# Two VectorE passes over neighbouring PSUM banks joined into one two-bank pass, with new planner seeds, in a scheduled attention and MLP kernel

## Chip, cores, metric

One core of a Trainium2 chip. The time is the device time of one execution in microseconds (us); medians of several executions are quoted. All executions here are fast (granted TensorE clock 0.997 to 1.0).

## The reference, cut

```python
def reference(A_x, A_wq, A_wk, A_wv, A_wo, B_x, B_w1, B_w2):     # x: 1 x 2048 x 512
    xn = _layernorm(A_x)
    q = (xn @ wq) as 32 heads of 16;  k = xn @ wk;  v = xn @ wv   # one k and v for all heads
    p = softmax(q k^T / 4);  s = (p v) @ wo
    g = silu(silu(xn @ w1) @ w2)                                 # F = 1792
    return x + s * g
```

## The kernel before

The kernel writes no instruction order by hand. A planner in Python places tasks on five engines one after another with assumed durations, and the instructions are emitted in the order found. What matters here:

- A **score phase** is up to four row-tiled score matmuls side by side, each filling one PSUM bank with a slot of 128 keys x 512 (head, query) columns. Seven banks rotate.
- A slot goes one of two ways. ScalarE takes the exp of one to three neighbouring banks in one call, and TensorE then needs one probability-times-V matmul. Or VectorE makes 16-bit exponents from one bank (the "pass"), GpSimd makes three shifted copies of them, and TensorE needs four such matmuls. So VectorE relieves ScalarE and loads TensorE.
- Between score phases TensorE does column-tiled work in rounds of four matmuls: P times V, the MLP, projections.
- Random numbers from ten seeds vary some limits of the planner. The seeds decide the order, and are picked for a good result.

```python
SEEDS, STRETCH, SPREAD = (2502, 4652, 1398, ...), 64, 0.3
...
        def pass_d(b, bt, g, i, kt):                 # one slot on VectorE
            tot[g, i] += K
            def placed(pop):
                pool_free.append(b)                  # the bank may be planned again
                pvq[g][i].append(...)                # and the slot's P times V
            bt.P[i] = pl.add(Task(DV, T_P, lambda v: v.tensor_scalar(
                db_sb[:, bt.b, i * NQ:(i + 1) * NQ], bank(b), 128.0 * LOG2E, 128.0 * (SHIFT_BETA + 127.0),
                op0=ALU.mult, op1=ALU.add), [("ps", b)], [("Db", bt.b, i)], 0, on_place=placed))
...
        def do_S(t):                                 # one score phase
            banks = [b for r, b in bank_times() if r <= t + 30][:4]
            ...                                      # dslots for VectorE, sl for ScalarE
            for b, d in zip(dbanks, dslots):
                pass_d(b, *d)
```

The softmax here doesn't subtract the row's maximum and nothing guards it: scores larger than these inputs give would overflow.

## Time and profile before

| | before |
|---|---|
| time, median of 2 | 669.83 us |
| span of the profiled run | 668.0 us |
| busy TensorE, ScalarE, VectorE, GpSimd | 99%, 98%, 92%, 84% |
| score phases / passes on VectorE | 640 / 736 |

Two lines besides those that the prediction shows. The group of score matmuls (columns: line, engine, operation, count; busy us and mean ns; idle time before them and who ended it):

```profile
L866 PE MATMUL ps<-qt_sb,kt_sb 32*128 32x512 bf16 x2048 | 250.7, 384 | 3.7 <-ACT pa_sb L1717 1.1 <-DVE db_sb L1002 0.5 <-DVE kt_sb L567 0.4
```

And the last score phase in the timeline (start us, length us):

```profile
657.37 0.10 PEld L866 LDWEIGHTS ps<-qt_sb,kt_sb 32*128 32x128 bf16 x3 [0.42 <-issue]
```

The steady stretch thus ends at 657.4 us, and 10.6 us of tail follow.

### The profile page before, as it was taken

What the parts mean: (1) busy time and instruction counts of PE and PEld (TensorE: products, weight loads), DVE (VectorE), ACT (ScalarE), POOL (GpSimd) and SP (SyncE); (2) the same over time, 40 slices, a digit from 0 to 9 for tenths busy, and PEclk for the clock granted to TensorE, in tenths of its full rate; (3) what the DMA queues carried; (4) which work ended last, traced back from release to release, by engine and by line L of the source; (5) the groups of instructions that cost most, each with busy time, mean ns of one, the idle gap of its engine ahead of it and who ended that gap; (6) DMA issues with size and microseconds to landing.
All of it is one profiled execution on the core that took longest, in us unless ns stands there. A gap on an engine that the chain in (4) does not pass through costs nothing.

```text
span 668.0 us, 21223 instructions
## 1 busy us (share of the span) xinstructions
PE 658.0 (99%) x8962; PEld 191.2 (29%) x8963; DVE 615.0 (92%) x1093; ACT 652.1 (98%) x768; POOL 558.7 (84%) x556
## 2 busy tenths in 40 slices
PE   8999999999999999999999999999999999999997
PEld 4422222222222222222222222222222222222223
DVE  8989999899999998999998999999899999998995
ACT  6999999999999999999999999999999999999996
POOL 3059889989898899898899887999899989998972
PEclk9999999999999999999999999999999999999999
DMA  8500000000000000000000000000000000000000
GB/s 299 166 9 2 2 2 2 2 3 2 1 2 18 19 18 18 1 2 2 2 2 2 17 18 18 18 2 1 3 2 2 2 18 17 18 18 2 2 2 33
DMA packets 11821, 12.86 MB, mean 19 GB/s; under 512 B 1808, under 2 KB 11216, under 8 KB 11728
## 3 DMA queue, kind: packets, MB, share of 16 engines
q1 hardware_dynamic: 10928, 10.78, 5.0%
q8 instruction: 72, 1.18, 0.7%
q10 hardware_dynamic: 800, 0.72, 0.3%
q14 instruction: 21, 0.17, 0.1%
HBM read 8.95 MB, written 2.10 MB: 17 GB/s over the span
## 4 chain that ended last, share of the span: by engine, by line
PE 74%; ACT 17%; DVE 7%; issue 1%; DMA 0%; POOL 0%; ACTq 0%; DVEq 0%
PE ps L1282 32%; PE ps L866 25%; PE ps L511 16%; ACT pa_sb L1717 16%; DVE db_sb L1002 2%; ACT t_sb L669 1%; DVE stats_sb L458 1%; DVE u_sb L671 1%; DVE xnT_sb L538 0%; DMA ds_sb<-in_A_x_dram 0%; DVE xn_sb L487 0%; POOL ds_sb L1202 0%; DVE fin_sb L719 0%; DVE f_sb L1338 0%; DVE mv_sb L462 0%
## 5 line engine op out<-in xcount | busy, mean ns | idle before, releaser
L1202 POOL INT64_ADD ds_sb<-db_sb x544 | 553.1, 1038 | 91.6 <-DVE db_sb L1002 34.9
L1717 ACT ACTIVATE pa_sb<-ps 128x1024 bf16<-128x1024 f32 (+2 forms) x671 | 616.3, 1029 | 5.5 <-PE ps L866 3.1
L1002 DVE TENSOR_SCALAR db_sb<-ps 128x512 uint16<-128x512 f32 x736 | 475.5, 683 | 39.6 <-PE ps L866 28.6
L1282 PE MATMUL ps<-ds_sb,v_sb 128*32 128x512 bf16 x2208 | 274.4, 383 | 0.0
L866 PE MATMUL ps<-qt_sb,kt_sb 32*128 32x512 bf16 x2048 | 250.7, 384 | 3.7 <-ACT pa_sb L1717 1.1
L1282 PE MATMUL ps<-pa_sb,v_sb 128*32 128x512 bf16 x1317 | 245.8, 382 | 0.0
L1282 PE MATMUL ps<-db_sb,v_sb 128*32 128x512 bf16 x736 | 176.2, 383 | 0.0
L866 PEld LDWEIGHTS ps<-qt_sb,kt_sb 32*128 32x128 bf16 x2048 | 62.6, 90 | 275.6 <-ACT pa_sb L1717 154.5
L1282 PEld LDWEIGHTS ps<-ds_sb,v_sb 128*32 128x32 bf16 x2208 | 68.4, 95 | 60.4 <-issue 41.9
L511 PE MATMUL ps<-xnT_sb,w_sb 128*32 128x512 bf16 x896 | 71.9, 384 | 0.0
L1282 PEld LDWEIGHTS ps<-pa_sb,v_sb 128*32 128x32 bf16 x1317 | 60.7, 95 | 39.3 <-issue 26.7
L511 PE MATMUL ps<-w_sb,u_sb 128*32 128x512 bf16 x820 | 64.2, 384 | 0.0
L1282 PEld LDWEIGHTS ps<-db_sb,v_sb 128*32 128x32 bf16 x736 | 43.7, 95 | 20.3 <-issue 15.6
L669 ACT ACTIVATE t_sb<-ps 128x512 bf16<-128x512 f32 x72 | 45.2, 628 | 0.0
L671 DVE SCALAR_TENSOR_TENSOR u_sb<-t_sb,ps 128x512 bf16<-128x512 bf16 x56 | 38.3, 684 | 1.4
L618 PE MATMUL ps<-w_sb,u_sb 32*128 32x512 bf16 x76 | 29.2, 384 | 0.0
L511 PEld LDWEIGHTS ps<-xnT_sb,w_sb 128*32 128x32 bf16 x896 | 17.2, 94 | 27.3 <-issue 21.5
L511 PEld LDWEIGHTS ps<-w_sb,u_sb 128*32 128x32 bf16 x820 | 15.4, 95 | 23.0 <-issue 19.7
L1338 DVE STREAM_TRANSPOSE f_sb<-ps 128x512 f32<-128x512 f32 x31 | 21.9, 706 | 0.1
L511 PE MATMUL ps<-wo_sb,on_sb 128*32 128x512 bf16 x256 | 19.8, 383 | 0.3 <-DVE on_sb L1316 0.3
L511 PE MATMUL ps<-xnT_sb,wq_sb 128*32 128x512 bf16 x240 | 18.8, 384 | 0.0
L1342 DVE TENSOR_TENSOR otr_sb<-f_sb,rcp_sb 128x256 bf16<-128x256 f32 x31 | 12.9, 417 | 1.4 <-POOL ds_sb L1202 1.1
(75 smaller groups left out, 169.0 us busy)
## 6 DMA issues: line engine op xcount, KB each, us to landing
w_sb<-in_B_w_dram SPq DMA_DIRECT2D x2, 1792.0 KB, 14.3
xr_sb<-in_A_x_dram SPq DMA_DIRECT2D x16, 128.0 KB, 2.5
out_dram<-ob_sb SPq DMA_DIRECT2D x16, 128.0 KB, 1.7
ds_sb<-in_A_x_dram SPq DMA_DIRECT2D x3, 512.0 KB, 6.7
wq_sb<-in_A_wq_dram SPq DMA_DIRECT2D x1, 512.0 KB, 4.9
wo_sb<-in_A_wo_dram SPq DMA_DIRECT2D x1, 512.0 KB, 16.7
kt_sb<-kt_sb ACTq DMA_DIRECT2D x4, 112.0 KB, 4.2
ds_sb<-in_A_x_dram ACTq DMA_DIRECT2D x2, 128.0 KB, 2.9
```

What stands on the lines that cost most here:

```text
L458: ts_ = pl.add(Task(DV, 593.0, lambda v, t=t: v.bn_stats(stats_sb[:, t, :], x_tile(t)), [xkey(t)], [("st", t)], 1 + j, gate=(lambda j=j: S ...
L511: last = h.matmul(bank(b)[32 * j:32 * (j + 1), 0:n], lhsT=lhs(j), rhs=rhs, start=start, stop=stop, tile_position=(0, 32 * j), skip_group_c ...
L618: return (lambda pe: pe.matmul(bank(b), lhsT=lhs(k, rows, 0, P), rhs=rhs(k, rows), start=False, stop=last, tile_position=(32 * i, 0), skip ...
L669: t1 = Task(AC, 490.0, lambda a: a.activation(t_sb[:, k, :], src, ACT.Tanh, scale=scale), [held], [("t", k)], 0, [t0])
L671: t2 = Task(DV, T_P, lambda v: v.scalar_tensor_tensor(out=dst, in0=t_sb[:, k, :], scalar=1.0, in1=src, op0=ALU.add, op1=ALU.mult), [held, ...
L866: return pe.matmul(bank(b), lhsT=kt_sb[32 * i:32 * i + 32, g % 2, kt * P:(kt + 1) * P], rhs=qt_sb[32 * i:32 * i + 32, (g // 2) % NQR, :], ...
L1002: bt.P[i] = pl.add(Task(DV, T_P, lambda v: v.tensor_scalar(db_sb[:, bt.b, i * NQ:(i + 1) * NQ], bank(b), 128.0 * LOG2E, 128.0 * (SHIFT_BET ...
L1202: whole["po"].append(pl.add(Task(PO, T_P64, lambda g, cols=cols: g.int64_add(ds_sb[:, s, cols].bitcast(U64), db_sb[:, bt.b, cols].bitcast( ...
L1282: h = pe.matmul(bank(OB)[32 * i:32 * (i + 1), cols], lhsT=lhs, rhs=rhs, start=s0, stop=s1, tile_position=(0, 32 * i), skip_group_check=True)
L1338: t1 = pl.add(Task(DV, T_TR, lambda v: v.transpose(f_sb[:, k, :], bank(OB)), [("ps", OB)], [("F", k)], 1, [norm.get(("m", g - 2))]))
L1342: t3 = pl.add(Task(DV, 332.0, lambda v: v.tensor_tensor(o3[:, :, val:val + DH], f3[:, :, val:val + DH], rcp_sb[:, k, :].unsqueeze(2).to_br ...
L1717: op = pl.place(AC, 0.8333 * NQ * n + T_AF, lambda a: a.activation(pa_sb[:, s * NQ:(s + n) * NQ].rearrange("p (b n) -> p b n", n=NQ), ps3[ ...
```

## The change

The intent: VectorE pays a fixed amount per instruction. When a phase gives it two slots in neighbouring banks, one instruction reads both banks, and that amount is paid once. The seeds were changed in the same step, and the condition that starts the tail was made stricter. With joining off and the old seeds, the changed source builds into the same instructions, orders and waits as the kernel before, so the stricter condition does nothing there.

```diff
-SEEDS, STRETCH, SPREAD = (2502, 4652, 1398, 4134, 3319, 6151, 8548, 1413, 942, 5642), 64, 0.3
+SEEDS, STRETCH, SPREAD = (6371, 4628, 3818, 3584, 5044, 3525, 4965, 8747, 3685, 2283), 64, 0.3
+PAIR = 1
+        def pass_pair(b, ds):
+            bt, g = ds[0][0], ds[0][1]
+            ii = [d[2] for d in ds]
...
+            def placed(pop):
+                for k, (_, _, i, kt) in enumerate(ds):
+                    pool_free.append(b + k)
+                    pvq[g][i].append((pop, ...))
+            t = pl.add(Task(DV, 2 * T_P - 66.0, lambda v: v.tensor_scalar(
+                db_sb[:, bt.b, :].rearrange("p (i n) -> p i n", n=NQ)[:, ii[0]:ii[1] + 1:ii[1] - ii[0], :], ps3[:, b:b + 2, :],
+                128.0 * LOG2E, 128.0 * (SHIFT_BETA + 127.0), op0=ALU.mult, op1=ALU.add),
+                [("ps", b), ("ps", b + 1)], [("Db", bt.b, i) for i in ii], 0, on_place=placed))
...
-            for b, d in zip(dbanks, dslots):
-                pass_d(b, *d)
+            if PAIR and nd == 2 and dslots[0][0] is dslots[1][0] and dbanks[1] - dbanks[0] == 1:
+                pass_pair(dbanks[0], dslots)
+            else:
+                for b, d in zip(dbanks, dslots):
+                    pass_d(b, *d)
...                                        # and a stricter condition for make_tail()
```

More of the change, by code (lines that the diff above doesn't have):

```diff
@@ L1004, in pass_d @@
                 op0=ALU.mult, op1=ALU.add), [("ps", b)], [("Db", bt.b, i)], 0, on_place=placed))
+        def pass_pair(b, ds):
+            bt, g = ds[0][0], ds[0][1]
+            ii = [d[2] for d in ds]
+            for i in ii:
+                tot[g, i] += K
+            def placed(pop):
+                for k, (_, _, i, kt) in enumerate(ds):
+                    pool_free.append(b + k)
+                    pvq[g][i].append((pop, v_lhs(1, g, kt), db_sb[:, bt.b, i * NQ:(i + 1) * NQ].bitcast(BF16),
+                                      [("Db", bt.b, i)] + v_reads(1, kt), ("d", bt), None))
+            t = pl.add(Task(DV, 2 * T_P - 66.0, lambda v: v.tensor_scalar(
+                db_sb[:, bt.b, :].rearrange("p (i n) -> p i n", n=NQ)[:, ii[0]:ii[1] + 1:ii[1] - ii[0], :], ps3[:, b:b + 2, :],
+                128.0 * LOG2E, 128.0 * (SHIFT_BETA + 127.0), op0=ALU.mult, op1=ALU.add),
+                [("ps", b), ("ps", b + 1)], [("Db", bt.b, i) for i in ii], 0, on_place=placed))
+            for i in ii:
+                bt.P[i] = t
         def do_S(t):
@@ L1045, in do_S @@
             nd = len(dslots)
+            if PAIR and nd == 2 and dslots[0][0] is dslots[1][0]:
+                dslots.sort(key=lambda d: d[2])
             st["la"] = n - nd
@@ L1563, in pe_step @@
             start_jobs(t)
-            if st["assigned"] == NG * SLOTS and (MT_EARLY and not active and st["job"] == len(jobs) or st["expn"] == len(units)) and not tail["made"] and all(
+            if st["assigned"] == NG * SLOTS and (MT_EARLY and not active and st["job"] == len(jobs) and len(pool_free) + len(units) - st["expn"] == len(BANKS) or st["expn"] == len(units) and len(pool_free) == len(BANKS)) and not tail["made"] and all(
                     tt in tmp_task for tt in range(NT - 4, NT)):
```

## The prediction

> **What bounds the kernel now.** I read the engine totals first, then the busy time by stretches, then the groups kept apart by shape, then the waits, then the timeline of a steady piece.
>
> ```profile
> PE 658.0 (99%) x8962; PEld 191.2 (29%) x8963; DVE 615.0 (92%) x1093; ACT 652.1 (98%) x768; POOL 558.7 (84%) x556
> ```
>
> Three engines are nearly full, so the totals cannot say which one sets the time. From 38 to 657 us the split by stretches gives:
>
> ```profile
> 38.00:657.00 619.00, 617.39 (x8361) 172.19 (x8362) 576.51 (x960) 615.58 (x710) 553.06 (x544) 1.00 0.03 7
> ```
>
> The columns are length, then busy time of TensorE, weight loads, VectorE, ScalarE, GpSimd. TensorE and ScalarE both lack less than 4 us of 619; VectorE lacks 42 us, GpSimd 66 us. The head (38 us) and the tail (11 us) are short. TensorE's busy time is modelled, so I check it against the waits:
>
> ```profile
> PEld ps L866 <- ACT pa_sb L1717: 154.5, 364, 0.7
> PEld ps L866 <- DVE db_sb L1002: 102.4, 231, 0.8
> ```
>
> Line 866 is the score matmuls (row-tiled, one "phase" at a time), 1717 is ScalarE's exp, 1002 is VectorE's pass (scores in PSUM to 16-bit exponents), the line that the change touches. It looks as if TensorE lost 102 us to that pass. The timeline shows that it did not:
>
> ```profile
> 302.26 0.10 PEld L866 LDWEIGHTS ps<-qt_sb,kt_sb 32*128 32x128 bf16 x3 [0.42 <-ACT pa_sb L1717]
> 302.58 0.12 PEld L511 LDWEIGHTS ps<-xnT_sb,wq_sb 128*32 128x32 bf16 x8 [0.23 <-issue]
> 303.13 0.10 PEld L866 LDWEIGHTS ps<-qt_sb,kt_sb 32*128 32x128 bf16 x3 [0.42 <-ACT pa_sb L1717]
> ```
>
> The cycle is 303.13 - 302.26 = 0.87 us for one score phase and two rounds of column-tiled work. Three 512-column steps of 0.216 us are 0.65; the other 0.22 is two changes of tiling, about 0.11 each. A gap of 0.42 on the weight-load row is the last matmul streaming plus that change, not a wait. Going through the whole timeline in stretches of 4 us, 539 of 641 gaps before a score phase are exactly 0.42. Eighty exceed 0.44, by 6.5 us in all, and 5.0 of those 6.5 us stand behind the VectorE pass. **TensorE is the bound, and all its waiting before score phases is about 6.5 us, 1% of the span.**
>
> ScalarE is a close second:
>
> ```profile
> L1717 ACT ACTIVATE pa_sb<-ps 128x1024 bf16<-128x1024 f32 x624 | 591.0, 1051 | 4.4 <-PE ps L866 2.0 <-DVE rstd_sb L478 0.4 <-issue 0.3
> L1002 DVE TENSOR_SCALAR db_sb<-ps 128x512 uint16<-128x512 f32 x736 | 475.5, 683 | 39.6 <-PE ps L866 28.6 <-PE ps L618 5.4 <-POOL ds_sb L1202 1.2
> L1717 ACT ACTIVATE pa_sb<-ps 128x512 bf16<-128x512 f32 x41 | 24.7, 630 | 1.1 <-PE ps L866 1.0
> L1717 ACT ACTIVATE pa_sb<-ps 128x1536 bf16<-128x1536 f32 x6 | 8.7, 1485 | 0.0
> ```
>
> It idles 4.4 us before its 624 main calls. VectorE idles 39.6 us before its passes, mostly because the scores were not there yet.
>
> **What the Trainium skill says.** "VectorE: DVE Perf Modes", section "The TRN2 errata", puts an fp32 PSUM source at one element per cycle of 0.96 GHz and the measured fixed term of one operation at about 150 cycles: 533 + 156 = 689 ns for 512 elements. The trace's 683 agrees. But a duration is not a pitch. "Perfetto Trace Analysis", section "Optimizing Scalar/DVE Operations", says a PSUM operation's overhead as engine time is about 125 ns, the profiled latency being about twice that because the write acknowledgement overlaps the next instruction. Here the overlap is larger:
>
> ```profile
> 38.44 2.48 DVE L1002 TENSOR_SCALAR db_sb<-ps 128x512 uint16<-128x512 f32 x4
> ```
>
> Four passes in 2.48 us with the last 0.69 long: pitch (2.48 - 0.69) / 3 = 0.60 us, so the overhead per instruction is 600 - 533 = 67 ns. The measurement decides: joining two passes saves about 67 ns, not 125 or 150. "TensorEngine Tiling (Array Packing)", "Key Properties", says that changing the tiling mode drains the engine; the 0.11 us per change above agrees.
>
> **The change, part by part.** The order of both programs' instructions gives the counts; no time is in it.
>
> VectorE: 736 single passes become 616 single and 64 joined (40 with adjacent outputs, 24 with outputs strided by whole slots), so slots on VectorE go from 736 to 616 + 128 = 744. Joining saves 64 x 67 = 4.3 us. Eight more slots cost 8 x 0.60 = 4.8 us. Whole-batch shifts on VectorE fall from 8 to 4: 4 x 0.6 = 2.4 us less. Sum: about -1.9 us of 615, on an engine with some 40 us idle.
>
> GpSimd: shifts 544 to 554, 10 x 1.04 = +10.4 us, into 91.6 us of idle before them. Free.
>
> ScalarE: exp slots fall from 2048 - 736 = 1312 to 1304. From the rows (1485 - 630) / 1024 = 0.835 ns per element, so a slot is 0.427 us. A call on top costs, in engine time, about 65 ns (8 calls of 1024 took 7.44 us in the critical chain; less the last call's 1.05 that is 0.913 each, less 0.855). Calls, the half ones at the end included, go from 677 to 663. Saved: 8 x 0.427 + 14 x 0.065 = 4.3 us.
>
> TensorE, the bound: a slot done by exp needs one probability-times-V matmul, a slot done by VectorE needs four (the pass and three shifts). The order shows db 736 to 744, ds 2208 to 2232, pa (half ones at half) 1312 to 1304: +24. Eight more matmuls of the second product run as row-tiled pieces in spare score rows, which takes 2 rounds of four away, so rounds rise by 6 - 2 = 4, or 4 x 0.216 = 0.9 us. Rounding up each run of column work (unfilled rounds) it is 9 rounds, 1.9 us. Score phases fall from 640 to 638: 2 x (0.216 + 0.22) = -0.9 us. **Net TensorE work: 0 to +1.1 us.**
>
> So the joined pass frees the engine that is not the bound. What it can give is through the gaps: fewer waits of TensorE for banks. ScalarE's 4.3 us make its banks come free earlier, and VectorE's backlog is shorter. Against that stands the joined pass itself: it frees both banks at its end, 1.13 us after its start, where two passes freed the first at 0.60-0.69 and the second at 1.20-1.29. One bank is late by about half a microsecond, the other early by 67 ns, in 64 of 638 phases. I credit the gaps with 2 us of the 6.5. At the end the last score slots are exponentiated by column halves: before, each half was two calls of 2 x 256 columns and one of 256; now one and two. With 0.213 us per 256 columns and 0.065 a call that is 1.26 against 1.05 us a half, so 0.4 us less on the chain to the last store. Sum: +0.6 (middle of the TensorE work) - 2.0 - 0.4 = -1.8 us on 669.83, **668.0 us**.
>
> **The rivals.**
> First, *later banks eat it*: if each joined pass costs TensorE part of its half microsecond, say 0.06 us on average, 64 of them make 4 us and the time is about 672. For it: 5.0 of the 6.5 us of real waits already stand behind this pass. Against: the scheduler knows the joined pass as one task and places around it, seven banks rotate, and VectorE is often only waiting for scores.
> Second, *ScalarE was the true limit and TensorE's work was stretched to it*: then the 4.3 us come off in full, plus the tail, and the time is 665. For it: 98% busy with 4.4 us idle. Against: 539 score phases start at the minimum gap, so TensorE has hardly anything to give back.
> Third, *the fixed cost of a pass was worth its face value*: 64 x (2 x 683 - 1223) = 9 us off, 661. Against: the pitch shows 67 ns, and VectorE has idle time.
> Fourth, *only the new seeds matter*: they reshuffle every choice after the first 40 us, so the result may differ by a microsecond or two either way for no reason of the joined pass.
>
> **Range and chances.** The rivals that I believe reach from 665 to 672; the seeds' own scatter lies inside. I take 664.8 to 671.0. A change of 2% is 13.4 us: more than twice all waits of TensorE before score phases, so faster by over 2% would need work that is not removed; slower by over 2% would need 0.2 us per joined pass, which the scheduler would have avoided. Chances: faster 0.02, same 0.97, slower 0.01.
>
> **What would show the steps right or wrong.** The joined pass should last about 1.22 us (683 + 533) with a pitch near 1.13, alike with adjacent and strided outputs; if it lasts twice 683 the saving is none. Busy sums take whole durations: VectorE should fall by about 6.6 us (120 x 0.683 + 4 x 0.688 less 64 x 1.22), ScalarE by about 6 (5 x 1.051 + 15 x 0.630 less 6 x 1.485), GpSimd rise by about 10. TensorE should stay at 99%, and the gaps of score phases above 0.42 should sum to 4 to 5 us. If they sum to over 8, the late banks decided. If TensorE still waits as now and the span falls by over 4 us, my count of rounds is wrong. Wrong altogether: a span that leaves 663 to 669.2 (the range less the 1.8 us between the time and the span).

## The result, and the profile after

The changed kernel takes 673.13 us (median of 2), **3.3 us more**; ratio 1.0049, 95% interval 1.0029 to 1.0069. Ratios are the mean time of one kernel's fast runs over that of the other's of the same rounds, so not quite the ratio of the medians quoted. The difference is far below 2%, but clear of the noise. In a second session five runs gave 672.93 against 669.83.

Engine totals after, to set against the first line of the prediction:

```profile
PE 658.9 (98%) x8985; PEld 192.9 (29%) x8986; DVE 611.5 (91%) x1033; ACT 649.7 (97%) x754; POOL 568.8 (85%) x566
```

VectorE has 3.6 us less to do and ScalarE 2.4 less; the span grew all the same. The groups by shape:

```profile
L1741 ACT ACTIVATE pa_sb<-ps 128x1024 bf16<-128x1024 f32 x619 | 586.3, 1052 | 9.1 <-PE ps L867 6.6 <-DVE rstd_sb L479 0.4 <-issue 0.3
...
L1003 DVE TENSOR_SCALAR db_sb<-ps 128x512 uint16<-128x512 f32 x616 | 402.5, 683 | 37.7 <-PE ps L867 23.4 <-PE ps L619 9.1 <-POOL ds_sb L1226 1.8
...
L1018 DVE TENSOR_SCALAR db_sb<-ps 128x1024 uint16<-128x1024 f32 x64 | 77.7, 1218 | 3.1 <-PE ps L867 1.2 <-POOL ds_sb L1226 0.5
```

The joined pass (L1018) does what was said of it, 1218 ns. But ScalarE's idle time before its main calls went from 4.4 to 9.1 us, now mostly behind the score matmuls (L867): TensorE brings scores later. The end of the steady stretch shows it:

```profile
660.52 0.09 PEld L867 LDWEIGHTS ps<-qt_sb,kt_sb 32*128 32x128 bf16 x2 [0.42 <-issue]
```

The last score phase starts at 660.52 instead of 657.37. All of the loss, 3.15 us, lies before it; the tail is 10.6 us in both. I read the weight-load rows of the whole timeline in stretches of 4 us and paired them with the program's order, so that every gap and every round is counted:

| from the last work of the head to the last score phase | before | after | us |
|---|---|---|---|
| score phases x 0.433 | 623 | 621 | -0.9 |
| rounds of column work, unfilled ones counted, x 0.216 | 1579 | 1589 | +2.2 |
| gaps before score phases above 0.42 us | 6.5 us | 6.7 us | +0.2 |
| gaps before column work above 0.23 us | 0.6 us | 2.1 us | +1.6 |
| sum | | | +3.1 |

Of the ten rounds five are matmuls really added, in steps of a quarter round (1575.75 to 1580.75), the other five are rounds begun with fewer than four matmuls because nothing else was ready. The two largest new gaps before column work, 0.6 us each beyond the usual, look like this in the timeline:

```profile
66.06 1.22 DVE L1018 TENSOR_SCALAR db_sb<-ps 128x1024 uint16<-128x1024 f32 x1
...
67.19 0.71 DVE L1362 STREAM_TRANSPOSE f_sb<-ps 128x512 f32<-128x512 f32 x1
...
67.95 0.11 PEld L1306 LDWEIGHTS ps<-db_sb,v_sb 128*32 128x32 bf16 x6 [0.87 <-DVE f_sb L1362]
```

The accumulator bank is freed by a transposing copy on VectorE, and this one stands behind a joined pass. The other large gap, at 374.03, waits for the same copy with no joined pass just before it, so the reading does not hold for both. Nor does the joined instruction itself make the first one. In split_after below, the same order with single passes, it is longer, and in single_newseeds, with no joining at all, gaps of this kind stand too (first line split_after, second single_newseeds):

```profile
68.22 0.12 PEld L1337 LDWEIGHTS ps<-db_sb,v_sb 128*32 128x32 bf16 x6 [1.00 <-DVE f_sb L1393]
409.99 0.10 PEld L1306 LDWEIGHTS ps<-db_sb,v_sb 128*32 128x32 bf16 x4 [0.84 <-DVE f_sb L1362]
```

These gaps belong to the orders. The profile alone cannot tell whether joining or the new seeds made this order; the runs do.

### The profile page after: what moved, and what is told of

It is laid out like the page before. It is cut to its first block, busy times and chain, and to the rows that moved or that the text cites. A ratio compares the mean times of both kernels' runs of the same rounds, so it can differ in the third digit from the quotient of the medians.

```text
span 671.1 us, 21168 instructions
## 1 busy us (share of the span) xinstructions
PE 658.9 (98%) x8985; PEld 192.9 (29%) x8986; DVE 611.5 (91%) x1033; ACT 649.7 (97%) x754; POOL 568.8 (85%) x566
## 4 chain that ended last, share of the span: by engine, by line
PE 56%; ACT 8%; DVE 1%; issue 0%; ACTq 0%; DVEq 0%
PE ps L1306 24%; PE ps L867 18%; PE ps L512 13%; ACT pa_sb L1741 8%; DVE db_sb L1003 1%; ACT t_sb L670 1%; PE ps L1527 0%; DVE fin_sb L720 0%; DVE u_sb L672 0%; ACT ob_sb L1532 0%; ACTq L328 0%; DVE ob_sb L732 0%; PE ps L619 0%; DVEq L289 0%; ACTq L289 0%
## 5 line engine op out<-in xcount | busy, mean ns | idle before, releaser
L1226 POOL INT64_ADD ds_sb<-db_sb x554 | 563.1, 1038 | 87.4 <-DVE otr_sb L1366 31.7
L1003 DVE TENSOR_SCALAR db_sb<-ps 128x512 uint16<-128x512 f32 x616 | 402.5, 683 | 37.7 <-PE ps L867 23.4
L1306 PE MATMUL ps<-ds_sb,v_sb 128*32 128x512 bf16 x2232 | 259.6, 383 | 0.0
L867 PE MATMUL ps<-qt_sb,kt_sb 32*128 32x512 bf16 x2048 | 250.0, 384 | 4.4 <-ACT pa_sb L1741 1.1
L1306 PE MATMUL ps<-pa_sb,v_sb 128*32 128x512 bf16 (+1 forms) x1308 | 230.9, 383 | 0.0
L1306 PE MATMUL ps<-db_sb,v_sb 128*32 128x512 bf16 x744 | 165.2, 383 | 1.1 <-DVE f_sb L1362 1.1
L867 PEld LDWEIGHTS ps<-qt_sb,kt_sb 32*128 32x128 bf16 x2048 | 62.5, 91 | 273.9 <-ACT pa_sb L1741 148.8
L1306 PEld LDWEIGHTS ps<-ds_sb,v_sb 128*32 128x32 bf16 x2232 | 65.6, 95 | 62.1 <-issue 43.5
L1018 DVE TENSOR_SCALAR db_sb<-ps 128x1024 uint16<-128x1024 f32 x64 | 77.7, 1218 | 3.1 <-PE ps L867 1.2
L1306 PEld LDWEIGHTS ps<-pa_sb,v_sb 128*32 128x32 bf16 x1308 | 57.6, 95 | 41.2 <-issue 27.7
L1306 PEld LDWEIGHTS ps<-db_sb,v_sb 128*32 128x32 bf16 x744 | 40.3, 95 | 22.2 <-issue 15.2
L619 PE MATMUL ps<-w_sb,u_sb 32*128 32x512 bf16 x84 | 32.3, 385 | 0.0
```

What stands on the lines that cost most here:

```text
L619: return (lambda pe: pe.matmul(bank(b), lhsT=lhs(k, rows, 0, P), rhs=rhs(k, rows), start=False, stop=last, tile_position=(32 * i, 0), skip ...
L867: return pe.matmul(bank(b), lhsT=kt_sb[32 * i:32 * i + 32, g % 2, kt * P:(kt + 1) * P], rhs=qt_sb[32 * i:32 * i + 32, (g // 2) % NQR, :], ...
L1003: bt.P[i] = pl.add(Task(DV, T_P, lambda v: v.tensor_scalar(db_sb[:, bt.b, i * NQ:(i + 1) * NQ], bank(b), 128.0 * LOG2E, 128.0 * (SHIFT_BET ...
L1018: t = pl.add(Task(DV, 2 * T_P - 66.0, lambda v: v.tensor_scalar(db_sb[:, bt.b, :].rearrange("p (i n) -> p i n", n=NQ)[:, ii[0]:ii[1] + 1:i ...
L1226: whole["po"].append(pl.add(Task(PO, T_P64, lambda g, cols=cols: g.int64_add(ds_sb[:, s, cols].bitcast(U64), db_sb[:, bt.b, cols].bitcast( ...
L1306: h = pe.matmul(bank(OB)[32 * i:32 * (i + 1), cols], lhsT=lhs, rhs=rhs, start=s0, stop=s1, tile_position=(0, 32 * i), skip_group_check=True)
```

## The experiments

Three theories. **A**: the joined pass frees its first bank later than a single pass would, and that costs, either at once on the chip or in the order that the planner must choose. **B**, a part of A: once the order is chosen, nothing is lost directly. **C**: joining is neutral, and the new seeds brought a worse order. Each session ran the kernel before beside the others; its median was 669.73 to 669.88 each time.

| run | order | passes | late bank | median us | ratio to before (95%) |
|---|---|---|---|---|---|
| after_again | new seeds | joined | yes | 672.93 | 1.0046 (1.0033 to 1.0059) |
| split_after | as after | single | no | 675.02 | 1.0077 (1.0063 to 1.0091) |
| fuse_before | as before | 43 joined | yes | 677.43 | 1.0114 (1.0100 to 1.0128) |
| hold_before | as before | single | 43 times | 677.98 | 1.0126 (1.0112 to 1.0140) |
| fuse_slack | as before | 28 joined | only where not due | 670.18 | 1.0003 (0.9990 to 1.0015) |
| pair_oldseeds | old seeds | joined | yes | 680.52 | 1.0157 (1.0143 to 1.0171) |
| held_oldseeds | old seeds | single | yes | 680.92 | 1.0167 (1.0153 to 1.0181) |
| single_newseeds | new seeds | single | no | 674.24 | 1.0064 (1.0049 to 1.0080) |
| single_r1 / pair_r1 | random seeds 1 | single / joined | no / yes | 672.57 / 679.13 | 1.0043 / 1.0140 |
| single_r2 / pair_r2 | random seeds 2 | single / joined | no / yes | 676.12 / 683.37 | 1.0096 / 1.0204 |

All results were correct.

### Orders kept, passes changed

The first four ran on one chip, fuse_slack later on another. To keep an order, the finished plan is taken and every wait is worked out again from what each operation reads and writes:

```diff
+        seq = []
+        for op, reads, writes, after, ports in pl.seq:   # as planned
+            ...                                          # split or join passes here
+            seq.append((op, reads, writes, after, ports, op))
+        pl.replay(seq)                                   # same order, new waits
```

**after_again**, the changed kernel as it is.

> The changed kernel once more, on the chip of the three runs that follow, so that the split version has a neighbour to stand against. All theories: 673.1 us give or take 0.5, ratio to before 1.005.

It came out at 672.93, as expected.

**split_after**, the order of the changed kernel, passes single again:

```diff
+            b, db, ii = pl.tags[id(op)]                  # a joined pass: two in its place
+            for k, i in enumerate(ii):
+                o.emit = lambda v, b=b + k, db=db, i=i: v.tensor_scalar(db_sb[:, db, i * NQ:(i + 1) * NQ], bank(b), ...)
+                seq.append((o, [("ps", b + k)], [("Db", db, i)], after, ports, op))
```

> The changed kernel with every engine's order kept, but each of the 64 joined passes issued as two single passes of one bank each, so that the first bank is free about 0.5 us earlier and the second 0.06 us later. Theory A (the late bank holds TensorE up directly, on the chip): 1 to 3 us faster than the changed kernel, 670 to 672. Theory B (the cost is in the order that the scheduler chose because of the late bank; once chosen it stays): within 0.7 us of the changed kernel, 672.5 to 673.8, with the same 638 score phases. Rival C (the new seeds alone): as B.

675.02, so 2.1 us **slower** than the changed kernel, which neither theory had expected. My reading: in an order made for joined passes the first bank is not needed early, and what counts is when the second is free, so part of the 64 x 67 ns now comes due. Gaps above 0.44 us before score phases rise from 74 to 92 and their excess from 6.7 to 8.8 us, all of it behind VectorE's passes. So inside its own order joining is a gain of 2.1 us, and direct waits do not explain the 3.3 us.

**fuse_before**, the order of the kernel before, 43 pairs joined:

```diff
+        for o1, o2 in zip(pl.order[DV], pl.order[DV][1:]):    # neighbours on VectorE, of one phase and batch
+            ...                                               # banks next to each other, no use of the second slot between
+            fused[id(o1)] = o2                                # o1 becomes the joined pass, o2 goes
```

> The kernel before with its order kept on every engine, but 43 pairs of neighbouring single passes (same phase, neighbouring banks) made into joined ones. Theory A: each joined pass costs TensorE about 0.05 us directly, so 1 to 4 us slower than before, 671 to 674. Theory B: within 0.7 us of before, 669.3 to 670.5, because in a fixed order most banks are freed well ahead of their next use. If the 67 ns saved on VectorE were worth anything by themselves: up to 1 us faster.

677.43, **7.6 us slower**, more than even A expected. The same place in the timeline, before:

```profile
61.33 3.19 DVE L1002 TENSOR_SCALAR db_sb<-ps 128x512 uint16<-128x512 f32 x5
...
63.39 0.10 PEld L866 LDWEIGHTS ps<-qt_sb,kt_sb 32*128 32x128 bf16 x3 [0.53 <-DVE db_sb L1002]
```

and with the pair joined:

```profile
62.71 1.23 DVE L1817 TENSOR_SCALAR db_sb<-ps 128x1024 uint16<-128x1024 f32 x1
63.99 0.10 PEld L896 LDWEIGHTS ps<-qt_sb,kt_sb 32*128 32x128 bf16 x3 [1.06 <-DVE db_sb L1817]
```

The next score phase needs the first of the two banks as soon as it is free. It starts right after the joined pass ends, 0.60 us later; 0.07 of these were lost earlier, and the gap is 0.53 longer. Twelve gaps of this kind (0.97 to 1.07 us where 0.42 is usual) have an excess of 7.4 us. The group of score matmuls agrees (here against 3.7 us before):

```profile
L896 PE MATMUL ps<-qt_sb,kt_sb 32*128 32x512 bf16 x2048 | 250.8, 384 | 10.3 <-DVE db_sb L1817 7.2 <-ACT pa_sb L1750 1.1 <-DVE kt_sb L597 0.4
```

Both programs have the same TensorE order, so their weight-load rows can be laid side by side, one by one. Twelve score phases lose 0.52 to 0.56 us each against the kernel before, 6.4 us together (part of their excess was there already). Three more places, two of them before column work, lose 0.2 to 0.3 us each. The remaining 0.4 us is spread thinly. So the cost is not 0.18 us in each of 43 places; it falls in fifteen of them.

**hold_before**, order and instructions of the kernel before, only the late bank added:

```diff
+            if id(op) in self.held:
+                k, o2 = self.held[id(op)]        # the first pass's bank, the second pass
+                self.readers[k].append(o2)       # TensorE may reuse the bank after the second only
```

> The kernel before with order and instructions kept, and only one wait added in the same 43 places: TensorE may reuse the first bank of the pair only after the second single pass (the late bank without the joining). Theory A: as fuse_before or slower by 43 x 0.06 at most, 671 to 675. Theory B: within 0.7 us of before. The difference to fuse_before is the worth of 43 x 67 ns on VectorE: under 1 us.

677.98: two single passes with the late bank are as slow as joined ones. Its group of score matmuls:

```profile
L900 PE MATMUL ps<-qt_sb,kt_sb 32*128 32x512 bf16 x2048 | 250.8, 384 | 11.1 <-DVE db_sb L1039 8.1 <-ACT pa_sb L1754 1.1 <-DVE kt_sb L601 0.4
```

Again twelve long gaps, each some 0.06 us longer than with the joined pass (8.2 us of excess against 7.4); laid beside the kernel before, each loses 0.60 us, and the same three further places lose some too. **The late bank is the cause of the loss in this order, and the saved 67 ns are worth 0.5 us of 8.** Theory B is wrong for an order that was not made for joined passes.

**fuse_slack**, as fuse_before, but only pairs whose first bank and slot are not due before the joined pass has ended:

```diff
+            end = o1.t0 + 2 * T_P - 66.0 + LAT[DV, PE]
+            use = [o.t0 for o, r, w, _, _ in later if o.eng == PE and (bank of o1 in w or slot of o1 in r)]
+            if use and min(use) < end + 50.0:
+                continue
```

> As fuse_before (order of the kernel before kept), but only those 28 of the 43 pairs are joined where, in the plan, no work of TensorE on the first bank or slot begins before the joined pass has ended. Theory A sharpened (a joined pass costs about 0.65 us where its first bank is due at once and nothing elsewhere): 669.3 to 670.3, level with before, and a dozen score-phase gaps near 1.1 us gone. Rival (joining costs something in itself, whatever is due): 28/43 of 7.6 us, so 674 to 675.

670.18 against 669.88: level. The 15 pairs left out are the very ones behind which fuse_before lost time: there, each delayed row starts 0.05 to 0.11 us after the joined pass ends. All gaps above 0.9 us are gone, and the joined passes are as long as elsewhere:

```profile
L897 PE MATMUL ps<-qt_sb,kt_sb 32*128 32x512 bf16 x2048 | 250.8, 384 | 3.8 <-ACT pa_sb L1751 1.1 <-DVE kt_sb L598 0.4 <-DVE db_sb L1036 0.3
L1822 DVE TENSOR_SCALAR db_sb<-ps 128x1024 uint16<-128x1024 f32 x28 | 34.2, 1221 | 1.7 <-PE ps L897 0.8
```

Neither a joined instruction nor the replay costs anything in itself, and 28 x 67 ns = 1.9 us taken from VectorE gained nothing either. This was the best hope for a version that beats both kernels, and it does not beat the kernel before.

### Scheduled anew

**pair_oldseeds** takes the changed kernel with the old seeds; **held_oldseeds** replaces the joined pass there by two single ones, whose banks the planner gets back together; **single_newseeds** switches joining off and keeps the new seeds.

```diff
 pair_oldseeds:    -SEEDS ... = (6371, 4628, ...)   +SEEDS ... = (2502, 4652, ...)
 single_newseeds:  -PAIR = 1                        +PAIR = 0
 held_oldseeds:    old seeds, and in pass_pair
+            for k, (_, _, i, kt) in enumerate(ds):
+                def placed1(pop, k=k, i=i, kt=kt):
+                    if k == 1:
+                        pool_free.extend((b, b + 1))
+                    pvq[g][i].append(...)                  # each slot as its own pass ends
+                bt.P[i] = pl.add(Task(DV, T_P, ..., [("ps", b), ("ps", b + 1)][:k + 1], [("Db", bt.b, i)], 0, first[-1:], on_place=placed1))
```

> The changed kernel with the seeds of the kernel before: the joining alone, scheduled anew. Theory A (late banks cost, and only the choice of seeds hid most of it): well slower than the changed kernel, 678 to 684. Rival C (the joining is neutral and the new seeds cost the 3.3 us): 669 to 671.

680.52, 10.7 us slower than the same seeds with single passes (which is the kernel before). Theory C is out: joining is not neutral. With joining on, the new seeds are 7.4 us faster than the old ones, and so **hide** 7.4 of the 10.7.

> Seeds of the kernel before, two single passes instead of a joined one, but the scheduler gets both banks back only after the second: the late bank alone, scheduled anew. Theory A: as slow as pair_oldseeds within 4 us, 678 to 685. If the joined instruction itself were what costs: near 670.

680.92. With the planner free to choose, the late bank without any joining is as slow as joining, within 0.4 us. That the two agree so closely is partly chance, for the orders differ (60 held pairs here, 86 joined ones there). In the profile, 7.4 us of the loss lie before the last score phase and 4.8 us in the tail, against 10.95 and -0.2 in pair_oldseeds; the profiled run was 1.1 us slower than the median.

> The changed kernel with joining switched off and the new seeds kept: the seeds alone. Theory A: the seeds were picked for joined passes, so for single ones they are as any seeds: 671 to 677. Rival C: 672.5 to 674, equal to the changed kernel. By itself this run does not tell the theories apart; with pair_oldseeds it does.

674.24. As the expectation says, alone it decides nothing. It does show that with the new seeds joining is slightly better (673.13 and 672.93 against 674.24): the seeds fit joined passes, as the old ones fit single passes. It also means that the 3.3 us cannot be shared out. By one path joining costs 10.7 and the new seeds give back 7.4; by the other the new seeds cost 4.4 and joining gives back 1.1.

Where do 10.7 us go when the planner is free? In pair_oldseeds the last score phase starts at 668.3 us, 10.95 later than before. The order has 631 phases instead of 640 (-3.9 us) and 27 more rounds of column work, unfilled ones counted (+5.8 us). VectorE holds 752 slots instead of 736, and each slot moved there costs TensorE three more matmuls, 12 rounds in all. Another 7.5 rounds are filler matmuls on zeros, which the planner issues when TensorE has little else:

```profile
L512 PE MATMUL ps<-zer_sb 128*32 128x256 bf16 x132 | 5.8, 275 | 0.0
```

against 72 before. Waits add to it: gaps before score phases hold 10.5 us of excess instead of 6.5, those before column work 3.0 instead of 0.6. These terms add up to 8.3 us; 2.6 of the 10.95 stay unaccounted for. One loss thus seems to show in several places: later banks, then fewer ready inputs, more slots moved to VectorE, unfilled rounds, fillers. Which of these follows from which is read from counts and not shown by a run of its own.

### Random seeds

Two sets of ten random seeds, nothing picked, joining off and on.

```diff
-SEEDS, STRETCH, SPREAD = (6371, 4628, 3818, ...), 64, 0.3
+SEEDS, STRETCH, SPREAD = (ten random numbers), 64, 0.3
```

> First set of ten random seeds, single passes. It is the neighbour of pair_r1. Any theory: 670 to 677, slower than before, whose seeds were picked.

> The same random seeds with joining on. Theory A (with seeds not picked for it, joining costs, as it did with the old seeds): 4 to 12 us slower than single_r1. If the 10.7 us of the old seeds were an accident of seeds that had been picked for single passes: as often faster as slower, within 3 us of single_r1.

672.57 and 679.13: joining costs 6.6 us.

> Second set of random seeds, single passes: 670 to 679 by any theory.

> The second random seeds with joining on. Theory A: 4 to 12 us slower than single_r2. If an accident of seeds: within 3 us of single_r2 either way.

676.12 and 683.37: joining costs 7.3 us. With the old seeds it was 10.7, with the seeds picked for it -1.1 to -1.3. Only two random sets were run, so 7 us is no more than their middle; but the sign is the same in all three sets that had not been picked for joining (the old seeds had been picked for single passes).

The planner keeps a clock of its own, from its assumed durations. Where this clock ends was read by building the kernels without a chip; these are plans and not measurements (us):

| seeds | plan, single | plan, joined | measured, single | measured, joined |
|---|---|---|---|---|
| old | 663.6 | 674.8 | 669.8 | 680.5 |
| new | 668.1 | 667.6 | 674.2 | 673.1 |
| random 1 | 665.8 | 674.0 | 672.6 | 679.1 |
| random 2 | 670.6 | 678.2 | 676.1 | 683.4 |

Joining costs 11.1, -0.5, 8.3 and 7.6 us in the plans, and 10.7, -1.1, 6.6 and 7.3 us on the chip. So where the planner works anew, the loss is already in the order that it finds. The change, old single to new joined, is +3.9 in the plans and +3.3 measured.

## Why the prediction was wrong

I said 668.0, 664.8 to 671.0; it was 673.1. The bound, the counts and the durations held; the sign of the effect on waits did not. By term, the 5.1 us of error are: gaps before score phases 2.2, gaps before column work 1.6, TensorE's work 0.7, the tail 0.3, and 0.3 of rounding and of the step from span to time.

- **TensorE is the bound**: right. The 3.1 us of the account are all on TensorE.
- **The joined pass's length and pitch**: right. 1218 ns against 1.22, the same for adjacent and strided outputs in one group; all but one of the passes that follow a joined one directly start 1.13 to 1.14 us after it.
- **VectorE, ScalarE, GpSimd**: right. I had added up whole durations, and so added up VectorE falls by 7.1 us where I had 6.6, ScalarE by 5.8 where I had about 6. The page's busy times count overlapping instructions once and fall by 3.6 and 2.4. GpSimd's rose by 10. None of this is on the bound, and fuse_slack shows that spare VectorE time bought nothing in the old order.
- **Net TensorE work, 0 to +1.1 us, taken as 0.6**: a little too small. In the steady stretch it is +1.3.
- **"I credit the gaps with 2 us of the 6.5": the step that failed.** The gaps before score phases did not shrink by 2.0 us but grew by 0.2. Gaps before column work, for which the sum had no term, grew by 1.6. Together this is 3.8 of the 5.1 us. One sentence earlier I had written down what makes joining costly: one bank is late by half a microsecond, the other early by 67 ns. I weighed it against ScalarE's and VectorE's shorter work. hold_before measures the late bank alone: +8.2 us in a fixed order, 0.60 us in each of twelve places and less in three more, out of 43. With the planner free, joining costs 6.6 to 10.7 us with seeds not picked for it. In the changed kernel itself this is not a direct wait (split_after is slower still); it is in the order. Which step of the planner made each of its new gaps stays open.
- **The tail, -0.4 us**: wrong in size. It was 10.65 us and 10.57; the half-exps changed as counted, but the tail got only 0.1 shorter.
- **The first rival, later banks, about 672**: right in kind, wrong in form. I spread it as a direct 0.06 us over 64 passes; in the fixed order it is mostly 0.53 us where the bank is due at once, and nothing in 28 of 43 places. In the changed kernel's own order joining is even a gain of 2.1 us. Its sign, gaps over 8 us, did not come either (6.7). That its 672 lies near 673.1 is therefore luck. My argument against it, that the planner places around the joined pass, was true and no comfort: placing around it costs 6.6 to 10.7 us, and only seeds picked for it brought the change down to 3.3.
- **The fourth rival, the seeds, one or two us either way**: too small. Single passes alone range from 669.8 to 676.1 over four sets of seeds. The small change measured is the sum of two larger ones of opposite sign, +10.7 for joining and -7.4 for seeds by the one path, +4.4 for seeds and -1.1 for joining by the other.

## What to carry to other kernels

Joining two instructions that free buffers saves one fixed cost (67 ns here) and frees the first buffer only at the end of both. Before counting the saving, look how often the bound engine takes the first buffer at once; each such place cost 0.53 us here, nearly the 0.60 us of a whole second pass. And where a planner with picked seeds decides the order, a comparison needs both arms with the same seeds, or both picked: two runs with seeds exchanged told more here than the timing of the change. Where a planner keeps a clock, read it before predicting: counting the instructions of both orders showed one microsecond of work, while the planned ends were 3.9 us apart.

## What the Trainium skill lacked or had wrong

- "Perfetto Trace Analysis", "Optimizing Scalar/DVE Operations", gives some 125 ns of overhead as engine time for a VectorE instruction on PSUM. In back-to-back passes here it was 67 ns (pitch 0.60 us for 512 fp32 elements, and 1.13 to 1.14 for 1024; taking off 533 ns per 512 elements; the two durations here differ by 535).
- The same section says that larger operations help if the engine is saturated, and that smaller ones may help where the engine is not saturated but causes bubbles elsewhere. The second applies here, and I had read only the first: VectorE is 92% busy. The page has no size for it; the runs give about 0.53 us of TensorE time for most places where the first bank is due, 7.6 us for 43 joined pairs.
- "TensorEngine Tiling (Array Packing)", "Key Properties", says that a change of tiling mode drains the engine, without a figure. Here it was about 0.11 us per change (an estimate, from the 0.87 us cycle in the prediction), which leaves a 0.42 us gap on the weight-load row before each score phase that is easily taken for a wait.
- "VectorE: DVE Perf Modes", "The TRN2 errata": a fixed term of about 150 cycles puts one and two banks at 689 and 1223 ns; measured 683 and 1218. The page measured that term on SBUF operands, and its row for a PSUM source has 120 cycles, 658 and 1192 ns, which is shorter than the durations here. The page could say that its 150 holds for PSUM sources too.
